# Head of a fused attention and gMLP kernel: block 0 on two queues, K's weights ahead of the first DMA transposes, row sums from a scalar operation

## The chip, the cores and the metric

The kernel runs on one core of a Trainium2 chip. The metric is the device time of one execution in microseconds (us). Lower is better. In this text PE is the matrix engine, DVE the vector engine, ACT the scalar engine, POOL the GpSimd engine and SP the sync engine, which here does nothing but issue DMAs.

## The reference

The input x has 2048 rows of 512 values in bf16. It is normalised row by row, and two branches that read the normalised rows are added to it:

```python
def _A_ref(x, wqkv, wo):                      # H = 32 heads of 16, W = 8 taps, dilation 2
    qkv = (x @ wqkv).reshape(B, S, 3, H, Dh)  # -> q, k, v per head
    idx = pos[:, None] - off[None, :]         # off = 0, 2, ..., 14
    logits = einsum('bhsd,bhswd->bhsw', q, k[idx]) * Dh ** -0.5   # masked where idx < 0
    o = einsum('bhsw,bhswd->bhsd', softmax(logits), v[idx])
    return o @ wo

def _B_ref(x, w_in, w_sp, b_sp, w_out):       # F = 1792, Fh = 896
    z = gelu(x @ w_in)
    z1, z2 = z[..., :Fh], layernorm(z[..., Fh:])
    g = einsum('ts,bsf->btf', w_sp, z2) + b_sp[None, :, None]
    return (z1 * g) @ w_out

xn = layernorm(x)
return x + _A_ref(xn, wqkv, wo) + _B_ref(xn, w_in, w_sp, b_sp, w_out)
```

## The kernel before

The rows are cut into 16 blocks of 128, numbered 0 to 15, and into 4 groups of 512. Every step of the work is a task with an engine, a function that issues its instructions, an assumed duration `est` and the keys that it reads and writes. A planner in the kernel (`Plan.schedule`) walks through the tasks with a model of the engines and gives each engine one fixed order. It uses the `est` values, a model of DMA (`dma_bw`, `dma_lat`), assumed landing times for the first loads (`land`), a tolerance `tol` within which a task of better priority may go first, and `overlap`, the time by which a DVE instruction may start before its predecessor's end. `emit` then writes each engine's instructions in that order with semaphore waits. The order of the first tasks is written out by hand, as lists of names before the call of `plan.schedule` (L1006 to L1015): each name in a list follows the one before it.

The stages, by their lines and task names:

- **Loads.** `ldx0` to `ldx15` bring the blocks of x (L541, L514), `ldwv0` and `ldwv1` the two halves of V's weights (L518), `ldwin2a0`, `ldwin2a1` (L524) and `ldwin2b` (L530) the columns of w_in that make z2, `ldq` and `ldk` the weights of Q and K (L536). A queue issues its DMAs in order. Block 0, block 1 and `ldwin2a0` are issued by ACT, the rest by SP.
- **Warm-up.** `NWARM` matmuls of ones (L561) keep PE busy until the first data are there. Eight have 512 columns, the rest 128.
- **Blocks 0 and 1.** They are not normalised before their first use. DVE sums each row (`sum0`, `sum1`, L592) and subtracts the mean (`cen0`, `cen1`, L594), PE transposes the result (`xTc0_0` to `xTc1_1`, L578), ACT copies it to SBUF (L599), and V and z2 of these blocks are scaled by 1/std as they leave PSUM.
- **Layernorm of every block.** `bnst` (L603), `bnag` (L605) and `vpe` (L609) on DVE, `rstd` on POOL (L621), `norm` on DVE (L637).
- **Transposes of the normalised rows.** Blocks 2 and 3 go through PE (`xTr2`, `xTr3`, L578) and an ACT copy (L627). Blocks 0, 1 and 4 to 15 go by DMA transposes issued on SP (`xTd`, L631).
- **Projections.** V (`V`, L666; its ACT copy L670 and its store by POOL L673), z2 (`z2_b_0`, `z2_b_1`, L770, with its gelu on ACT L775 and sums of squares L780), Q and K (`Qj_c`, `Kj_c`, L682, with the ACT copy L691), z1 (L813).
- **Attention on DVE.** Products (L703, L708), softmax (L733 to L757), products with V (`pv`, L938, L941, L944) and a DMA transpose of each block's result (`OTd`, L947).
- **Spatial mixing and output.** g on PE (L910), its ACT copy (L918) and two DVE operations (L921, L924), then for each block the two output products on PE (L966, L975), the residual on DVE (L981) and the store (L986). For block 15 the output is cut in two parts.

On SP the hand-written order before is `ldq`, `xTd0`, `xTd1`, `ldk`, `ldx8` to `ldx15`. On DVE it is `sum0`, `cen0`, `sum1`, `cen1`, the statistics of blocks 0, 2 and 1, `norm2`, the statistics of block 3, `norm0`, `norm1`, `norm3`. On PE the first projection of Q, `Q0_0`, follows `z2_3_1`.

Of the kernel before, what the change touches and what calls it, by code (L numbers as in the profile page):

```python
# [10 lines left out]
ALU = mybir.AluOpType  # L11
ACTF = mybir.ActivationFunctionType
AX = mybir.AxisListType
# [325 lines left out]
def build_kernel(nc, A_x, A_wqkv, A_wo, B_x, B_w_in, B_w_sp, B_b_sp, B_w_out, out, report=False, emit=True):  # L339
# [3 lines left out]
    NB = S // 128  # L343
# [5 lines left out]
    NVS = 4  # L349
    NPB = 3  # L350
    NXT = 4
    NWARM = 15
    x2 = A_x[0]
    o2 = out[0]

# [3 lines left out]
    off = {}  # L359
# [34 lines left out]
    plan = Plan()  # L394

    with ExitStack() as es:
        ar = es.enter_context(nc.sbuf_tensor("arena", [128, AR], BF))
# [19 lines left out]
        def P(bk, n, o_=0):  # L417
            return ps[:, bk.col(o_): bk.col(o_) + n]
# [62 lines left out]
        def c_act(n, psum=True, accum=False):  # L481
            return (170.0 if psum else 205.0) + n * 0.833 + (200.0 if accum else 0.0)
# [4 lines left out]
        def c_ts(n):  # L487
            return 265.0 + n * 0.27

        T = plan.add  # L490

        def dma(eng, fn, nbytes, chan, reads=(), writes=(), name="", xbar=False, prio=0.0, after=()):
            return T(eng, fn, reads=reads, writes=writes, name=name, prio=prio, after=after,
                     dma=dict(chan=chan, nbytes=nbytes, xbar=xbar))
# [12 lines left out]
          writes=["ident"], est=300, name="ident1")  # L507
# [4 lines left out]
        def ld_x(b, eng="sp"):  # L512
            sl = b
            return dma(eng, lambda e: e.dma_start(A("xin", 512, 512 * sl), x2[128 * b:128 * b + 128, :]), 128 * 512 * 2,  # L514
                ("xin", sl), writes=[("xin", sl)], name="ldx%d" % b)

        def ld_wv(hf):
            dma("sp", lambda e: e.dma_start(AC(off["wv"] + 1024 * hf, [[512, 2], [1, 512]]),  # L518
                                            A_wqkv[256 * hf:256 * hf + 256, 1024:1536].rearrange("(c p) n -> p c n",
                                                                                               p=128)),  # L520
                256 * 512 * 2, ("wv", hf), writes=[("wv", hf)], name="ldwv%d" % hf)

        def ld_win2a(kh, eng):
            dma(eng, lambda e: e.dma_start(  # L524
                AC(off["w_in2"] + 1792 * kh, [[896, 2], [1, 448]]),
                B_w_in[256 * kh:256 * kh + 256, 896:1344].rearrange("(c p) n -> p c n", p=128)),
                256 * 448 * 2, ("w_in2a", kh), writes=[("w_in2a", kh)], name="ldwin2a%d" % kh)
# [7 lines left out]
        def ld_wqk(which, eng):  # L535
# [2 lines left out]
                A_wqkv[:, 512 * which: 512 * which + 512].rearrange("(c p) n -> p c n", p=128)),  # L538
                512 * 512 * 2, ("wqk", which), writes=[("wqk", which)], name="ld%s" % ("qk"[which]))

        dma("act", lambda e: e.dma_start(A("xin", 512), x2[0:128, :]), 128 * 512 * 2, ("xin", 0),  # L541
            writes=[("xin0", 0), ("xin0", 1)], name="ldx0")
        ld_x(1, "act")
        ld_win2a(0, "act")
        ld_wv(0)
        ld_wv(1)
        ld_win2a(1, "sp")
        ld_x(2, "sp")
        ld_x(3, "sp")
        ld_win2b()  # L550
        ld_x(4, "sp")
# [5 lines left out]

        bw = plan.bank("warm")
        for wi in range(NWARM):
            n_ = 512 if wi < 8 else 128  # L560
            T("pe", (lambda bw, n_: lambda t: t.matmul(P(bw, n_), ones[:, 0:128], ones[:, 0:n_], start=True,  # L561
                                                       stop=True))(bw, n_),
              writes=[bw], est=(427.0 if n_ == 512 else 107.0), name="warm%d" % wi, prio=1000)
# [20 lines left out]
        def ln_block(b):  # L584
            sl = b % 8
            xin = A("xin", 512, 512 * b)
            xn = A("xn", 512, 512 * sl)
            xk = [("xin", b)] if b else [("xin0", 0), ("xin0", 1)]

            if b < 2:  # L590
                xc = A("xc", 512, 512 * b)
                T("dve", lambda v: v.tensor_reduce(Fv("sx", 1, b), xin, AX.X, ALU.add), reads=xk, writes=[("sx", b)],  # L592
                  est=685, name="sum%d" % b, prio=-2)
                T("dve", lambda v: v.tensor_scalar(xc, xin, 512.0, Fv("sx", 1, b), ALU.mult, ALU.subtract),  # L594
                  reads=xk + [("sx", b)], writes=[("xc", b)], est=c_ts(512), name="cen%d" % b, prio=-2)
                for hf in range(2):
                    bc = plan.bank("xTc%d_%d" % (b, hf))
                    pe_tr(xc, [("xc", b)], "xTc%d_%d" % (b, hf), bc, (2 * hf, 2 * hf + 1))
                    T("act", (lambda hf, bc: lambda a: a.activation(A("xcT", 256, 512 * b + 256 * hf),  # L599
                                                                    P(bc, 256, 256 * hf), ACTF.Copy,  # L600
                                                                    scale=1.0 / 512))(hf, bc),
                      reads=[bc], writes=[("xcT", b, hf)], est=c_act(256), name="xcT%d_%d" % (b, hf), prio=-1)
            T("dve", lambda v: v.bn_stats(Fv("st6", 6, 6 * b), xin), reads=xk, writes=[("st6", b)],  # L603
              est=685, name="bnst%d" % b, prio=b * 0.1)
# [225 lines left out]
        for b in range(2, NB):  # L830
# [7 lines left out]
          writes=[("KTpad", c) for c in range(4)], est=170, name="ktpad", prio=2, after=lnr[:8])  # L838
# [5 lines left out]
          prio=2, after=lnr[:8])  # L844
# [160 lines left out]
        byname = {t.name: t for t in plan.tasks}  # L1005
        for names in (["warm%d" % wi for wi in range(NWARM - 3)] + ["xTc0_0", "xTc0_1"] +  # L1006
                      ["warm%d" % wi for wi in range(NWARM - 3, NWARM)] +
                      ["V0_0", "xTc1_0", "xTc1_1", "V0_1", "V1_0", "V1_1", "z2_0_0", "z2_1_0", "z2_0_1", "xTr2",
                       "z2_1_1", "V2_0", "V2_1", "xTr3", "z2_2_0", "z2_2_1", "V3_0", "V3_1", "z2_3_0", "z2_3_1", "Q0_0"],
                      ("rstd2", "rstd1", "rstd3", "rstd4", "Vw0"), ["ldq", "xTd0", "xTd1", "ldk"] + ["ldx%d" % b for b in range(8, NB)],  # L1010
                      ("sum0", "cen0", "sum1", "cen1", "bnst0", "bnag0", "vpe0", "bnst2", "bnag2", "vpe2", "bnst1",
                       "bnag1", "vpe1", "norm2", "bnst3", "bnag3", "vpe3", "norm0", "norm1", "norm3", "bnst4"),
                      ["bnst%d" % b for b in range(4, NB)],
                      ("xcT0_0", "xcT0_1", "xcT1_0", "xcT1_1", "Ve0", "xTe2", "Ve1", "z2g0", "xTe3", "z2g1", "Ve2", "z2g2",
                       "z2s0"), ("V10_1", "Q3_3"), ("z2_3_1", "Q0_1"), ("z2_3_1", "Q0_2"), ("z2_3_1", "Q0_3")):  # L1015
            for n0, n1 in zip(names, names[1:]):
                if byname[n0] not in byname[n1].deps:
                    byname[n1].odeps.add(byname[n0])

        plan.schedule(tol=30.0, dma_bw=270.0, dma_lat=1300.0, overlap=0.0,  # L1020
                      land=dict(ldx0=3580.0, ldx1=4750.0, ldwv0=4100.0, ldwv1=5350.0, ldwin2a0=6550.0, ldwin2a1=6600.0, ldx2=7050.0, ldx3=7400.0,
                                ldwin2b=8650.0, ldx4=9050.0, ldx5=9400.0, ldx6=9750.0, ldx7=10200.0, ldq=11700.0,
                                ldk=15000.0))
        if report:
            print("arena", AR, "fp", FR)
            plan.report()
# [47 lines left out]
```

## Time and profile before

| what | value |
|---|---|
| median of 3 runs | 237.98 us (237.9 to 239.03) |
| the profiled execution | 238.3 us, span 237.1 us |
| PE busy | 231.5 us, 98% of the span |
| DVE busy | 215.8 us, 91% |
| ACT busy | 95.2 us, 40% |
| POOL busy | 32.1 us, 14% |
| DMA moved | 44.12 MB, mean 186 GB/s |

The span runs from the first to the last instruction of the program on the core. The profiled execution's own time is 1.2 us longer. All times in rows of the profile are counted from the span's start. A row of the trace's list in order of time gives the start, the duration, the engine, the line, the operation, its output and input, shapes and count, and in square brackets the idle time before it and what ended it. Instructions of one kind that follow each other are merged into a row. A queue that only issues is written with a q (SPq, ACTq, POOLq). Matmuls are pipelined: of 512 columns each has a duration of about 379 ns, but they start closer together than that.

### The profile page before, as it was taken

The page shows a single profiled execution, that of the slowest core. Times are in us where ns is not written, and L with a number is a line of the kernel's source. Part 1 is how long each engine was busy: PE and PEld are TensorE (multiplying, and loading weights), DVE is VectorE, ACT ScalarE, POOL GpSimd, SP SyncE. Part 2 cuts the span into 40 slices and gives each one's busy share as a digit, 9 for nine tenths or more (in the row PEclk, how much of TensorE's full clock was granted, in tenths as well). Part 3 has the DMA queues.
Part 4 walks back from the last instruction along what each step waited for, and adds up shares of the span by engine and source line. Part 5 has one row for each costly group of instructions (what it writes and reads, how often), then busy time and mean ns, then how long its engine had stood idle before and what let it go on. Part 6 is the DMA issues. An engine that isn't in the chain of part 4 may idle for free.

```text
span 237.1 us, 2958 instructions
## 1 busy us (share of the span) xinstructions
PE 231.5 (98%) x1109; PEld 108.5 (46%) x1130; DVE 215.8 (91%) x269; ACT 95.2 (40%) x141; POOL 32.1 (14%) x56
## 2 busy tenths in 40 slices
PE   8998999999999999999999999999999999999996
PEld 3444455555444444444444444444444444444443
DVE  4787989999997899999999999999989998999982
ACT  3496889988986896601113411111111111000000
POOL 1476381401634000000000000000000000000000
DMA  6979869998147239014299999999899866393443
GB/s 205 304 205 259 205 135 197 142 230 187 66 152 249 60 116 115 0 33 144 66 358 230 225 231 185 296 173 316 274 212 271 293 189 195 76 320 118 145 139 129
DMA packets 83117, 44.12 MB, mean 186 GB/s; under 512 B 55440, under 2 KB 82464, under 8 KB 83104
## 3 DMA queue, kind: packets, MB, share of 16 engines
q1 hardware_dynamic: 81600, 41.30, 70.7%
q0 software_dynamic: 800, 2.11, 2.3%
q10 hardware_dynamic: 704, 0.52, 0.7%
q8 instruction: 9, 0.15, 0.2%
q14 instruction: 4, 0.03, 0.1%
HBM read 26.35 MB, written 4.21 MB: 129 GB/s over the span
## 4 chain that ended last, share of the span: by engine, by line
PE 90%; DMA 4%; DVE 3%; issue 1%; SPq 1%; ACT 0%; POOL 0%; DVEq 0%
PE ps L910 41%; PE ps L682 11%; PE ps L813 10%; PE ps L975 10%; PE ps L770 8%; PE ps L966 6%; PE ps L666 4%; DMA arena<-in_A_x_dram 2%; DMA arena<-in_A_wqkv_dram 2%; DVE fpool L603 1%; ACT arena L775 0%; PE ps L718 0%; SPq L518 0%; DVE arena L981 0%; DVE fpool L605 0%
## 5 line engine op out<-in xcount | busy, mean ns | idle before, releaser
L910 PE MATMUL ps<-arena 128*128 128x512 bf16 x439 | 96.6, 379 | 0.5
L910 PEld LDWEIGHTS ps<-arena 128*128 128x128 bf16 x448 | 43.7, 98 | 53.1 <-issue 0.4
L918 ACT ACTIVATE arena<-ps 128x1024 bf16<-128x1024 f32 (+1 forms) x16 | 14.7, 916 | 75.3 <-PE ps L910 75.3
L703 DVE TENSOR_TENSOR arena<-arena 128x4096 bf16<-128x4096 bf16 x16 | 36.5, 2288 | 0.2
L938 DVE TENSOR_TENSOR arena<-arena 128x4096 bf16<-128x4096 bf16 x16 | 36.5, 2284 | 0.0
L941 DVE TENSOR_TENSOR arena<-arena 128x2048 bf16<-128x2048 bf16 (+1 forms) x32 | 30.6, 958 | 1.0
L682 PE MATMUL ps<-arena 128*128 128x512 bf16 x126 | 28.9, 379 | 1.3 <-DMA arena<-in_A_wqkv_dram 1.2
L708 DVE TENSOR_TENSOR arena<-arena 128x4096 bf16<-128x4096 bf16 x12 | 27.5, 2290 | 0.3
L975 PE MATMUL ps<-arena 128*128 128x512 bf16 (+2 forms) x117 | 26.9, 366 | 0.1
L770 PE MATMUL ps<-arena 128*128 128x448 bf16 x128 | 26.0, 352 | 0.0
L813 PE MATMUL ps<-arena 128*128 128x512 bf16 x110 | 24.4, 379 | 0.1
L682 PEld LDWEIGHTS ps<-arena 128*128 128x128 bf16 x128 | 14.3, 113 | 14.7 <-DMA arena<-in_A_wqkv_dram 1.7
L691 ACT ACTIVATE arena<-ps 128x1024 bf16<-128x1024 f32 x16 | 16.3, 1021 | 5.3 <-PE ps L682 5.0
L770 PEld LDWEIGHTS ps<-arena 128*128 128x128 bf16 x128 | 12.4, 98 | 11.7 <-DMA arena<-in_B_w_in_dram 0.2
L975 PEld LDWEIGHTS ps<-arena 128*128 128x128 bf16 x119 | 11.4, 98 | 12.8
L813 PEld LDWEIGHTS ps<-arena 128*128 128x128 bf16 x112 | 10.9, 98 | 13.3 <-ACT arena L819 0.3
L966 PE MATMUL ps<-arena 128*128 128x512 bf16 (+2 forms) x66 | 16.5, 366 | 0.1
L819 ACT ACTIVATE arena<-ps 128x1024 bf16<-128x1024 f32 (+1 forms) x16 | 13.9, 922 | 4.9 <-PE ps L813 4.9
L666 PE MATMUL ps<-arena 128*128 128x512 bf16 x60 | 15.2, 379 | 0.7 <-ACT arena L599 0.3
L780 ACT ACTIVATE arena<-arena 128x896 bf16<-128x896 bf16 x16 | 15.1, 946 | 0.1
L775 ACT ACTIVATE arena<-ps 128x896 bf16<-128x896 f32 x14 | 12.8, 915 | 3.3 <-PE ps L770 3.3
L981 DVE TENSOR_TENSOR arena<-ps,arena 128x512 bf16<-128x512 f32 (+2 forms) x17 | 10.4, 653 | 3.3 <-PE ps L975 2.8
(61 smaller groups left out, 168.8 us busy)
## 6 DMA issues: line engine op xcount, KB each, us to landing
arena<-vscr SPq DMA_DIRECT2D x16, 1024.0 KB, 6.0
arena<-in_A_x_dram SPq DMA_DIRECT2D x30, 128.0 KB, 4.1
vscr<-arena POOLq DMA_DIRECT2D x16, 128.0 KB, 2.3
out_dram<-arena SPq DMA_DIRECT2D x15, 128.0 KB, 2.0
arena<-in_A_wqkv_dram SPq DMA_DIRECT2D x2, 512.0 KB, 5.1
arena<-in_B_w_in_dram SPq DMA_DIRECT2D x1, 896.0 KB, 5.4
arena<-in_B_w_out_dram SPq DMA_DIRECT2D x1, 896.0 KB, 5.0
arena<-arena SPq DMA_TRANSPOSE x34, 2.9
```

The costliest lines, as they stand in the source:

```text
L666: last = t.matmul(P(bk, 512), xTv(b, dc), A("wv", 512, 512 * dc), start=(dc == 0), stop=(dc == 3))
L682: last = t.matmul(P(bk, 512, 512 * which), AC(off["wqk"] + 2048 * which + 512 * dc + c, [[4, 128]]), AC(off["xnT"] + dc * S + 512 * j, [[1 ...
L691: T("act", lambda a: a.activation(AC(qo, [[ko - qo, 2], [1, 512]]), P(bk, 1024).rearrange("p (t n) -> p t n", t=2), ACTF.Copy, scale=0.5), ...
L703: T("dve", (lambda pbv, qb, kb: lambda v: v.tensor_tensor(pbv, qb, kb, ALU.mult))(pbv, qb, kb), reads=rd, writes=[("pb", s_)], est=c_tt(40 ...
L708: T("dve", (lambda av, bv: lambda v: v.tensor_tensor(av, av, bv, ALU.add))(av, bv), reads=[("pb", 1)], writes=[("pb", acc)], est=c_tt(4096 ...
L770: last = t.matmul(P(bk, 448, 512 * hf), xTv(b, dc), AC(off["w_in2"] + 896 * dc + 448 * hf, [[1, 448]]), start=(dc == 0), stop=(dc == 3))
L813: last = t.matmul(P(bk, 512, 512 * i), AC(off["w_in1"] + 896 * dc + 128 * fc, [[1, 128]]), AC(off["xnT"] + dc * S + 512 * j, [[1, 512]]), ...
L910: last = t.matmul(P(bk, 512, 512 * i), AC(off["z2"] + FH * sh + 128 * fc, [[1, 128]]), AC(off["wT%d" % r_] + sh * 512, [[1, 512]]), start= ...
L938: T("dve", lambda v: v.tensor_tensor(tv, tv, av, ALU.mult), reads=[("attn", b)], writes=[("Vs", sv)], est=c_tt(4096), name="pv%d" % b, pri ...
L941: T("dve", (lambda n: lambda v: v.tensor_tensor(A("Vs", n, 4096 * sv), A("Vs", n, 4096 * sv), A("Vs", n, 4096 * sv + n), ALU.add))(n), wri ...
L966: last = t.matmul(P(bk, cn), AC(off["OT"] + 512 * tb + 128 * cc, [[1, 128]]), AC(off["wo"] + 512 * cc + c0, [[1, cn]]), start=(cc == 0), s ...
L975: last = t.matmul(P(bk, cn), AC(off["z1T"] + fc * S + 128 * tb, [[1, 128]]), AC(off["w_out"] + 512 * fc + c0, [[1, cn]]), start=False, sto ...
```

## The change

- Block 0's load is cut in two halves of 64 rows. `ldx0_0` is issued by ACT, `ldx0_1` by SP ahead of V's weights.
- `ldx2` is issued ahead of `ldwin2a1`.
- `sum0` and `sum1` are no longer a reduction. They are a multiply by one and an add of zero over the row, with the row's sum as second output. The first output goes to the tile that `cen0` and `cen1` then overwrite.
- `ldk` is issued right behind `ldq`, ahead of `xTd0` and `xTd1`.
- `norm0` moves up on DVE, from behind the statistics of block 3 to ahead of those of block 1. `rstd0` is named first in POOL's order.
- Two warm-up matmuls fewer: one of 512 columns and one of 128.
- The planner's numbers are new: `tol`, `dma_bw`, `dma_lat`, `overlap` and the assumed landing times.

```diff
-    NWARM = 15
+    NWARM = 13
...
-        dma("act", lambda e: e.dma_start(A("xin", 512), x2[0:128, :]), 128 * 512 * 2, ("xin", 0),
-            writes=[("xin0", 0), ("xin0", 1)], name="ldx0")
+        for hf, eng in ((0, "act"), (1, "sp")):
+            dma(eng, (lambda hf: lambda e: e.dma_start(ar[64 * hf:64 * hf + 64, off["xin"]: off["xin"] + 512],
+                                                       x2[64 * hf:64 * hf + 64, :]))(hf),
+                64 * 512 * 2, ("xin0", hf), writes=[("xin0", hf)], name="ldx0_%d" % hf)
         ld_x(1, "act")
         ld_win2a(0, "act")
         ld_wv(0)
         ld_wv(1)
+        ld_x(2, "sp")
         ld_win2a(1, "sp")
-        ld_x(2, "sp")
...
-            n_ = 512 if wi < 8 else 128
+            n_ = 512 if wi < 7 else 128
...
-                T("dve", lambda v: v.tensor_reduce(Fv("sx", 1, b), xin, AX.X, ALU.add), reads=xk, writes=[("sx", b)],
-                  est=685, name="sum%d" % b, prio=-2)
+                T("dve", lambda v: v.tensor_scalar(xc, xin, 1.0, 0.0, ALU.mult, ALU.add, accum_out=Fv("sx", 1, b)), reads=xk, writes=[("sx", b), ("xc", b)],
+                  est=410, name="sum%d" % b, prio=-2)
...
-                      ("rstd2", "rstd1", "rstd3", "rstd4", "Vw0"), ["ldq", "xTd0", "xTd1", "ldk"] + ["ldx%d" % b for b in range(8, NB)],
-                      ("sum0", "cen0", "sum1", "cen1", "bnst0", "bnag0", "vpe0", "bnst2", "bnag2", "vpe2", "bnst1",
-                       "bnag1", "vpe1", "norm2", "bnst3", "bnag3", "vpe3", "norm0", "norm1", "norm3", "bnst4"),
+                      ("rstd0", "rstd2", "rstd1", "rstd3", "rstd4", "Vw0"),
+                      ["ldq", "ldk", "xTd0", "xTd1"] + ["ldx%d" % b for b in range(8, NB)],
+                      ("sum0", "cen0", "sum1", "cen1", "bnst0", "bnag0", "vpe0", "bnst2", "bnag2", "vpe2", "norm0",
+                       "bnst1", "bnag1", "vpe1", "norm2", "bnst3", "bnag3", "vpe3", "norm1", "norm3", "bnst4"),
...
-        plan.schedule(tol=30.0, dma_bw=270.0, dma_lat=1300.0, overlap=0.0,
-                      land=dict(ldx0=3580.0, ldx1=4750.0, ldwv0=4100.0, ldwv1=5350.0, ldwin2a0=6550.0, ldwin2a1=6600.0, ldx2=7050.0, ldx3=7400.0,
-                                ldwin2b=8650.0, ldx4=9050.0, ldx5=9400.0, ldx6=9750.0, ldx7=10200.0, ldq=11700.0,
-                                ldk=15000.0))
+        plan.schedule(tol=5.0, dma_bw=250.0, dma_lat=1600.0, overlap=30.0,
+                      land=dict(ldx0_0=2700.0, ldx0_1=3050.0, ldx1=3650.0, ldwv0=4350.0, ldwv1=5250.0, ldwin2a0=6300.0,
+                                ldwin2a1=6850.0, ldx2=5800.0, ldx3=7250.0, ldwin2b=8400.0, ldx4=8750.0, ldx5=9100.0,
+                                ldx6=9450.0, ldx7=9800.0, ldq=11300.0, ldk=12800.0))
```

More of the change, by code (lines that the diff above doesn't have):

```diff
@@ L1009, in build_kernel @@
                        "z2_1_1", "V2_0", "V2_1", "xTr3", "z2_2_0", "z2_2_1", "V3_0", "V3_1", "z2_3_0", "z2_3_1", "Q0_0"],
-                      ("rstd2", "rstd1", "rstd3", "rstd4", "Vw0"), ["ldq", "xTd0", "xTd1", "ldk"] + ["ldx%d" % b for b in range(8, NB)],
-                      ("sum0", "cen0", "sum1", "cen1", "bnst0", "bnag0", "vpe0", "bnst2", "bnag2", "vpe2", "bnst1",
-                       "bnag1", "vpe1", "norm2", "bnst3", "bnag3", "vpe3", "norm0", "norm1", "norm3", "bnst4"),
+                      ("rstd0", "rstd2", "rstd1", "rstd3", "rstd4", "Vw0"),
+                      ["ldq", "ldk", "xTd0", "xTd1"] + ["ldx%d" % b for b in range(8, NB)],
+                      ("sum0", "cen0", "sum1", "cen1", "bnst0", "bnag0", "vpe0", "bnst2", "bnag2", "vpe2", "norm0",
+                       "bnst1", "bnag1", "vpe1", "norm2", "bnst3", "bnag3", "vpe3", "norm1", "norm3", "bnst4"),
                       ["bnst%d" % b for b in range(4, NB)],
-                      ("xcT0_0", "xcT0_1", "xcT1_0", "xcT1_1", "Ve0", "xTe2", "Ve1", "z2g0", "xTe3", "z2g1", "Ve2", "z2g2",
-                       "z2s0"), ("V10_1", "Q3_3"), ("z2_3_1", "Q0_1"), ("z2_3_1", "Q0_2"), ("z2_3_1", "Q0_3")):
+                      ("xcT0_0", "xcT0_1", "xcT1_0", "xcT1_1", "Ve0", "xTe2", "Ve1", "z2g0", "xTe3",
+                       "z2g1", "Ve2", "z2g2", "z2s0"), ("V10_1", "Q3_3"), ("z2_3_1", "Q0_1"), ("z2_3_1", "Q0_2"),
+                      ("z2_3_1", "Q0_3")):
             for n0, n1 in zip(names, names[1:]):
```

## The prediction

> **What bounds the kernel now.** I read the page first, then PE's waits, then the list in order of time around each wait.
>
> ```profile
> PE 231.5 (98%) x1109; PEld 108.5 (46%) x1130; DVE 215.8 (91%) x269; ACT 95.2 (40%) x141; POOL 32.1 (14%) x56
> ```
> ```profile
> PE ps L682 <- DMA arena<-in_A_wqkv_dram: 1.2, 1, 1.2
> PE ps L561 <- PEq L1059: 0.8, 1, 0.8
> PE ps L666 <- ACT arena L599: 0.3, 1, 0.3
> PE ps L666 <- issue: 0.2, 1, 0.2
> PE ps L666 <- ACT arena L775: 0.2, 1, 0.2
> ```
>
> PE bounds the whole span, and its work is fixed, so the time is that work plus PE's idle time. A row here gives total, count and longest. Of 2.7 us of waits, 1.2 are one wait of K's projection for K's weights. Apart from the last of them, all lie in the first 19 us, where this change works:
>
> ```profile
> 0.84 3.93 PE L561 MATMUL ps<-const-bfloat16-1.0 128*128 128x512 bf16 x12 [0.84 <-PEq L1059]
> ...
> 3.50 0.69 DVE L592 TENSOR_REDUCE fpool<-arena 128x1 f32<-128x512 bf16 x1 [2.31 <-DMA arena<-in_A_x_dram]
> ...
> 4.22 0.35 DVE L594 TENSOR_SCALAR arena<-arena,fpool 128x512 bf16<-128x512 bf16 x1
> ...
> 4.72 0.38 PE L578 MATMUL ps<-arena 128*128 128x128 bf16 x4
> ...
> 7.46 0.69 DVE L603 BATCH_NORM_STATS2 fpool<-arena 128x6 f32<-128x512 bf16 x1 [0.89 <-DMA arena<-in_A_x_dram]
> 7.62 2.43 PE L770 MATMUL ps<-arena 128*128 128x448 bf16 x12
> ...
> 9.03 0.58 PEld L770 LDWEIGHTS ps<-arena 128*128 128x128 bf16 x4 [0.18 <-DMA arena<-in_B_w_in_dram]
> ...
> 9.48 0.40 DVE L637 TENSOR_SCALAR arena<-arena,fpool 128x512 bf16<-128x512 bf16 x1
> ...
> 11.24 2.59 SPq L631 DMA_TRANSPOSE arena<-arena  x2
> 11.26 0.81 PE L666 MATMUL ps<-arena 128*128 128x512 bf16 x3 [0.16 <-issue]
> ...
> 12.12 0.23 PEld L578 LDWEIGHTS ps<-arena 128*128 128x128 bf16 x4 [0.55 <-DVE arena L637]
> ...
> 13.88 0.58 SPq L536 DMA_DIRECT2D arena<-in_A_wqkv_dram  x1
> ...
> 14.50 4.02 SPq L514 DMA_DIRECT2D arena<-in_A_x_dram  x8
> ...
> 16.25 1.03 PE L682 MATMUL ps<-arena 128*128 128x512 bf16 x4
> ...
> 18.45 3.86 PE L682 MATMUL ps<-arena 128*128 128x512 bf16 x17 [1.18 <-DMA arena<-in_A_wqkv_dram]
> ...
> 18.74 0.69 DVE L603 BATCH_NORM_STATS2 fpool<-arena 128x6 f32<-128x512 bf16 x1 [1.53 <-DMA arena<-in_A_x_dram]
> ```
>
> SP issues `ldk` only at 13.88, behind two transposes that wait for the late `norm0` and `norm1`; PE does `Q0_0` at 16.25 and then stands until 18.45.
>
> **The wait for K's weights.** How much PE loses there, and when `ldk` can land, come from these rows (PE's pace in a full stretch; DMA in four stretches):
>
> ```profile
> 26.22 7.07 PE L682 MATMUL ps<-arena 128*128 128x512 bf16 x32
> 33.13 6.22 PE L770 MATMUL ps<-arena 128*128 128x448 bf16 x32
> ```
> ```profile
> 2.00:2.75 0.75, 0.75 (x3) 0.30 (x2) 0.00 (x0) 0.52 (x1) 0.00 (x0) 1.00 0.67 205
> 2.75:5.50 2.75, 2.53 (x15) 1.23 (x13) 1.93 (x5) 1.44 (x4) 0.00 (x0) 1.00 0.98 326
> 5.50:11.00 5.50, 5.44 (x32) 2.56 (x32) 4.33 (x15) 2.16 (x6) 1.81 (x4) 1.00 1.06 349
> 11.00:12.40 1.40, 1.18 (x9) 0.59 (x10) 1.28 (x4) 1.40 (x3) 1.16 (x2) 1.00 0.07 23
> ```
>
> From 26.22 to 33.13 there are 32 matmuls, 0.216 us each. `Q0_0` is four, 0.86 us. From 16.25 to 18.45 are 2.20 us, so 1.34 us are lost. The last two numbers of each window are DMA's busy share and GB/s: saturated up to 11, almost idle (0.07) from 11.0 to 12.4. After the change `ldk` is issued right behind `ldq`, before that hole. Its 512 KB (0.524 MB) at 349 GB/s take 1.50 us; even started at the hole's end, 12.4, they land by about 13.9 where `K0_0` needs them at about 17.1 (16.25 + 0.86). The cover is 3 us, so the whole 1.34 us goes. SP issues one DMA more ahead (half of block 0, about 0.5 us by the x8 row, 4.02 / 8); DMA's saturation from 2.75 on hides that.
>
> What moves with it: `xTd0` and `xTd1` now queue behind 512 KB more, and `Q0_0` needs both. `norm0` now comes ahead of the row of 9.48, but `norm1` stays behind block 3's statistics, so `xTd1` is still issued near 11.2. Bounds for its landing: the 2.4 to 2.9 us of before and the up to 5.1 us that transposes took behind loads:
>
> ```profile
> DMA to landing us min/median/max: 2.4/2.6/2.9
> ```
> ```profile
> DMA to landing us min/median/max: 3.4/4.3/5.1
> ```
>
> The first row is the two at 11.24, the second three issued behind the eight loads of 14.50. That gives 13.6 to 16.3. I take 14.3, since only `ldk` is ahead, landed by 13.9. `Q0_0` will want to start at about 16.1, so it is covered; at the far end 0.2 us would be lost. The eight x loads follow at about 12.5 instead of 14.50; DVE's wait of 1.53 us at 18.74 goes too, which keeps DVE ahead of an earlier PE.
>
> **The start of block 0.** The split can only bring the landing forward from 3.50. The sum of a row as second output isn't in the trace. From below it is the plain scalar operation (L594), 0.35 us; from above the reduction (L592), 0.69, plus a read of the accumulator as ACT has it behind its own sums:
>
> ```profile
> 12.33 0.21 ACT L775 ACTIVATION_READ_ACCUMULATOR arena<-ps,fpool 128x1 f32 x1
> ```
>
> that is 0.35 to 0.90. I take 0.69: like the reduction it must add 512 values of a row. Anywhere in that range the step is worth little, because of what is late next. The Trainium skill's page "SBUF — State Buffer", section "Who interferes with whom", says that the form of this operation that also writes out its accumulator cannot enter the fast two-port modes; by that this step saves nothing, and no run here shows it. PE's start hangs on the chain load, sum, centre, transpose, V, and the two early ends of it can move by up to some 0.5 us together. But `z2_0_0` at 7.62 needs `ldwin2a1`, now behind `ldx2`, and `z2_0_1` needs `ldwin2b`:
>
> ```profile
> 1.82 0.46 SPq L524 DMA_DIRECT2D arena<-in_B_w_in_dram  x1
> ...
> 3.31 0.43 SPq L530 DMA_DIRECT2D arena<-in_B_w_in_dram  x1
> ```
> ```profile
> DMA to landing us min/median/max: 5.3/5.3/5.4
> ```
> ```profile
> DMA to landing us min/median/max: 5.7/5.7/5.7
> ```
>
> The landing rows are of these two issues. The first is `ldwin2a1`: 1.82 + 5.4 = 7.2. It changes places with block 2, which lands just before 7.46; so it will land there, 0.15 us before PE wants it now. The second is `ldwin2b`: 3.31 + 5.7 = 9.0. The weight load of 9.03 already waited for it by 0.18 us. The same bytes stand ahead of it after the change, so PE's head start is used up at 9.03. It survives only if all DMA runs earlier: from 2.00 to 2.75 the share is 0.67, so a fuller start gives at most 0.33 x 0.75 = 0.25 us. I take zero, range 0 to 0.25. With nothing of it gained and the sum at 0.90, the chain is 0.2 us late, which is what the waits of 11.26 and 12.12 absorb. The two warm-up matmuls left out only make room.
>
> **Block 2 ahead of `ldwin2a1`, `norm0` moved up.** The load for block 3's transpose stood idle 0.55 us at 12.12 behind DVE. On PE itself: three matmuls from 11.26 at 0.216 end at 11.91, and the next weights are loaded at 12.12, so 0.2 us is lost. DVE's chain to there begins with block 2 at 7.46 and is gapless. `ldx2` gains at most 224 KB at 349 GB/s, 0.66 us, at least about 0.1 (loads of both queues interleave); I take 0.55. `norm0` now lies in that chain, 0.40 us (the row of 9.48). `norm2` and all behind it: 0.15 us earlier, range -0.3 to 0.26. In the order of DVE `bnst1`, `bnag1`, `vpe1`, `norm2` wait behind `norm0`, and `norm0` for `rstd0`, which POOL has long done. Gain on PE: 0.15 us.
>
> **Sum.** 1.34 + 0 + 0.15 = 1.5 us (1.49). From the profiled 238.3 that gives 236.8; the median of 237.98 is 0.3 lower than the profiled time, so I predict 236.5. Own range of this case 236.0 (all of the 0.25, and 0.2 of the small waits) to 236.9 (block 2's chain 0.3 later). A change under 0.5%, 1.19 us, I call none, about what a measurement of this kernel can tell: the limits are 236.79 and 239.17.
>
> **Rivals.**
>
> *The head gives nothing.* Block 0 lands at 3.50 as before, because its halves share DMA engines that other loads fill, and `norm0` eats block 2's lead. For it: DMA is saturated from 2.75. Against it: it is not before that. Only K's 1.34 is left: 236.6. 10%. The Trainium skill's page "DMA: Bandwidth & Descriptors", section "Rules for kernel authors", has a rule for this: of two transfers to disjoint halves of the partitions it says "Don't bother", since both use the same engines. By it block 0 gains nothing.
>
> *Late transposes.* `Q0_0` takes over part of K's wait, for `xTd1`. For it: the 5.1 us row; if SP is held up by half a microsecond more behind its fuller queue, it lands at 16.9, 0.8 late: 237.3. Against it: `ldk` has landed well before. 10%.
>
> *A cold clock.* The first twelve warm-ups, eight of 512 columns and four of 128, took 3.93 us, 0.44 for each 512 columns, where later matmuls take 0.216: PE runs at half pace until about 4.7. If the earlier and thinner start puts that off by as long again, the 2.2 us of work from 4.72 to 7.62 (eight transposes of 128 columns at 0.054, eight V matmuls at 0.216) takes 2.2 us more, less 0.4 of waits there: 1.8 lost, about 238.3. 6%.
>
> *Slower: DVE's new order holds the last block.* PE's last product waits for the last DMA transpose of the attention result:
>
> ```profile
> 197.81 0.42 DVE L921 TENSOR_TENSOR arena<-arena 128x512 bf16<-128x512 bf16 x1 [0.50 <-ACT arena L918]
> ...
> 198.61 2.28 DVE L938 TENSOR_TENSOR arena<-arena 128x4096 bf16<-128x4096 bf16 x1
> ...
> 203.26 1.88 DVE L981 TENSOR_TENSOR arena<-ps,arena 128x512 bf16<-128x512 f32 x3
> ```
> ```profile
> 228.75 1.19 SPq L947 DMA_TRANSPOSE arena<-arena  x1
> ...
> 232.59 0.81 PE L966 MATMUL ps<-arena 128*128 128x384 bf16 x4
> ```
>
> It is issued at 228.75. With the 2.4 to 2.9 us of the transposes at 11.24 it lands at about 231.3; PE wants it at 232.59, a cover of 1.3 us. The planner's new `tol` and `overlap` order all later work anew, and 30 ns on each of 269 DVE instructions shift its model by up to 8 us. If one more product with V (198.61 to 203.26, 4.65 us) comes to lie behind 197.81, the transpose is 4.65 later, 3.3 beyond the cover: 236.5 + 3.3 = 239.8. It ends slower than before once more than 2.8 us (1.3 + 1.49) are moved there. Against it: DVE's idle times of 0.50 at 197.81 and 1.53 at 18.74 leave room, and DVE's later waits are for PE and ACT, which come earlier too. 14%.
>
> **How the numbers follow.** Forecast 60%, head nothing 10%, late transposes 10%, cold clock 6%, slower 14%. Faster by over 0.5%: 0.56 of the forecast's 0.60 and 0.06 of the 0.10 that lies at the limit, 0.62. Within: the 0.04 and 0.04 left, 0.10 and most of the clock's 0.06, 0.22. Slower: 0.14 and what is left of the clock, 0.16. The range from 235.8 (0.2 under the own range, for a run on the quick side) to 238.9 holds all cases but most of the slower one.
>
> **What would show it.** Right: `Q0_0` and `K0_0` without a gap; `ldk` landed before 14.5; the first z2 at 7.4 to 7.6 however early the first transposes are; the list of PE's waits after 20 us as short as now; the last OT transpose landed ahead of PE. Wrong: a wait of L682 for a transpose or L966 for a DMA; the second output under 0.5 or over 0.9 us makes its step wrong, not the sum; `z2_0_1` well before 9.0 makes the head's zero wrong.

## The result, and the profile after

The changed kernel takes 237.26 us (median of 22 runs, 236.94 to 239.26), the kernel before beside it 238.06 us. The ratio is 0.9969 [0.996, 0.9978]: shorter by 0.31%, about 0.75 us. The interval lies below 1, but the gain is under the 0.5% from which the prediction speaks of a change. The forecast was 0.63%, 1.49 us, so half of the gain is missing. The profiled execution takes 237.5 us with a span of 235.9; before it was 238.3 with 237.1. The span lost 1.2 us, the whole time only 0.8.

The page's row of engines after, and the list of PE's waits (us in total, times, longest):

```profile
PE 232.1 (98%) x1128; PEld 108.4 (46%) x1128; DVE 207.9 (88%) x271; ACT 94.8 (40%) x141; POOL 32.8 (14%) x56
```
```profile
PE ps L580 <- DVE arena L596: 0.9, 2, 0.4
PE ps L563 <- PEq L1063: 0.8, 1, 0.8
PE ps L668 <- ACT arena L601: 0.2, 1, 0.2
```

K's wait of 1.2 us is gone, and what the list of before had later in the span too. New are two waits of the transposes at the start (L580) for DVE's centred blocks. Lines behind L541 stand two higher than before. The list in order of time shows the start:

```profile
0.80 0.59 SPq L542 DMA_DIRECT2D arena<-in_A_x_dram  x1
...
0.81 0.57 ACTq L542 DMA_DIRECT2D arena<-in_A_x_dram  x1
...
1.43 0.84 ACTq L514 DMA_DIRECT2D arena<-in_A_x_dram  x1
1.44 1.08 SPq L518 DMA_DIRECT2D arena<-in_A_wqkv_dram  x2
...
3.52 0.69 DVE L594 TENSOR_SCALAR_CACHE_REDUCE arena<-arena 128x512 bf16<-128x512 bf16 x1 [2.32 <-DMA arena<-in_A_x_dram]
...
4.06 0.44 SPq L530 DMA_DIRECT2D arena<-in_B_w_in_dram  x1
...
4.13 0.08 DVE L594 DVE_READ_ACCUMULATOR arena<-arena 128x1 f32 x1
4.25 0.35 DVE L596 TENSOR_SCALAR arena<-arena,fpool 128x512 bf16<-128x512 bf16 x1
...
5.38 0.69 DVE L594 TENSOR_SCALAR_CACHE_REDUCE arena<-arena 128x512 bf16<-128x512 bf16 x1 [0.78 <-DMA arena<-in_A_x_dram]
...
6.52 0.40 PE L580 MATMUL ps<-arena 128*128 128x128 bf16 x4 [0.42 <-DVE arena L596]
...
8.22 1.25 PEld L772 LDWEIGHTS ps<-arena 128*128 128x128 bf16 x8 [0.40 <-DMA arena<-in_B_w_in_dram]
8.23 2.51 PE L772 MATMUL ps<-arena 128*128 128x448 bf16 x12
...
9.80 0.49 PEld L772 LDWEIGHTS ps<-arena 128*128 128x128 bf16 x4 [0.33 <-DMA arena<-in_B_w_in_dram]
...
16.63 7.07 PE L684 MATMUL ps<-arena 128*128 128x512 bf16 x32
...
233.44 0.55 PE L977 MATMUL ps<-arena 128*128 128x128 bf16 x7
```

Block 0 is there no earlier than before: DVE starts on it at 3.52 (before 3.50). Both halves took 0.57 to 0.59 us to issue, block 1's load behind them 0.84, and everything further back in both queues goes out later: `ldwin2b` (L530) at 4.06 instead of 3.31. Block 1's sum starts at 5.38 after a wait for its load (before at 4.49 without a wait), the first z2 at 8.23 (before 7.62), and `Q0_0` at 16.63, 0.38 us later than before. From there all 32 matmuls of Q and K are one row of 7.07 us: no gap. The rows of before for block 1's load and its sum:

```profile
1.26 0.46 ACTq L514 DMA_DIRECT2D arena<-in_A_x_dram  x1
...
4.49 0.68 DVE L592 TENSOR_REDUCE fpool<-arena 128x1 f32<-128x512 bf16 x1
```

The stretches of DMA (us, busy share and GB/s are the last two numbers) show a hole after, between 3.0 and 3.5, that before does not have; after comes first:

```profile
3.00:3.50 0.50, 0.50 (x3) 0.23 (x2) 0.00 (x0) 0.50 (x1) 0.00 (x0) 1.00 0.59 111
```
```profile
3.00:3.50 0.50, 0.50 (x3) 0.22 (x2) 0.00 (x0) 0.50 (x1) 0.00 (x0) 1.00 1.06 367
```

The account goes by three marks: `Q0_0`'s start, the last product's row on PE, and the time around the span (a run's time less its span). The row of before:

```profile
234.60 0.55 PE L975 MATMUL ps<-arena 128*128 128x128 bf16 x7
```

- Up to `Q0_0`: 16.25 to 16.63, 0.38 us lost. The first z2 is 0.61 late; from it to `Q0_0` it is 8.40 us instead of 8.63, so 0.23 come back.
- From there to the last row: 218.35 (234.60 - 16.25) to 216.81 (233.44 - 16.63), 1.54 gained: 1.34 of K's wait and 0.20 of small waits, such as that for L775.
- Around the span: median of the 22 runs 1.57 us, beside 1.2 before; 0.3 to 0.4 lost.

Together 0.8, the difference of the two profiled executions.

### The profile page after: what moved, and what is told of

It reads as the page before. It is cut to its first block, busy times and chain, and to the rows that moved or that the text cites. A ratio compares the mean times of both kernels' runs of the same rounds, so it can differ in the third digit from the quotient of the medians.

```text
span 235.9 us, 2986 instructions
## 1 busy us (share of the span) xinstructions
PE 232.1 (98%) x1128; PEld 108.4 (46%) x1128; DVE 207.9 (88%) x271; ACT 94.8 (40%) x141; POOL 32.8 (14%) x56
## 4 chain that ended last, share of the span: by engine, by line
PE 96%; DMA 2%; DVE 1%; ACTq 0%; issue 0%; DVEq 0%
PE ps L912 41%; PE ps L684 12%; PE ps L772 10%; PE ps L815 10%; PE ps L977 10%; PE ps L668 6%; PE ps L968 6%; DMA arena<-in_A_x_dram 2%; PE ps L720 1%; DVE arena L983 0%; PE ps L580 0%; DVE arena L594 0%; ACTq L542 0%; DVE arena L596 0%; DVEq L319 0%
## 5 line engine op out<-in xcount | busy, mean ns | idle before, releaser
L684 PEld LDWEIGHTS ps<-arena 128*128 128x128 bf16 x128 | 14.5, 113 | 13.0
L983 DVE TENSOR_TENSOR arena<-ps,arena 128x512 bf16<-128x512 f32 (+2 forms) x17 | 11.1, 657 | 10.0 <-PE ps L977 10.0
L693 ACT ACTIVATE arena<-ps 128x1024 bf16<-128x1024 f32 x16 | 16.3, 1021 | 5.9 <-PE ps L684 5.7
L923 DVE TENSOR_TENSOR arena<-arena 128x1024 bf16<-128x1024 bf16 (+1 forms) x16 | 10.0, 624 | 7.7 <-ACT arena L920 7.7
L668 PE MATMUL ps<-arena 128*128 128x512 bf16 x64 | 16.1, 380 | 0.2 <-ACT arena L601 0.2
L821 ACT ACTIVATE arena<-ps 128x1024 bf16<-128x1024 f32 (+1 forms) x16 | 13.9, 919 | 4.9 <-PE ps L815 4.7
```

The source lines that it names most:

```text
L668: last = t.matmul(P(bk, 512), xTv(b, dc), A("wv", 512, 512 * dc), start=(dc == 0), stop=(dc == 3))
L684: last = t.matmul(P(bk, 512, 512 * which), AC(off["wqk"] + 2048 * which + 512 * dc + c, [[4, 128]]), AC(off["xnT"] + dc * S + 512 * j, [[1 ...
L693: T("act", lambda a: a.activation(AC(qo, [[ko - qo, 2], [1, 512]]), P(bk, 1024).rearrange("p (t n) -> p t n", t=2), ACTF.Copy, scale=0.5), ...
```

## The experiments

Where a ratio is given it is to the kernel before, run beside it on the same chip.

**K's order alone**, on the kernel before (`k_order`):

```diff
-["ldq", "xTd0", "xTd1", "ldk"]
+["ldq", "ldk", "xTd0", "xTd1"]
-ldk=15000.0
+ldk=13400.0
```

> The kernel before, with K's weights issued ahead of the first two DMA transposes and nothing else changed (PE's and DVE's orders stay as they were). Theory A (K's wait is the whole gain of the change and the start gives some of it back): PE's gap before the first K matmuls goes from 1.34 us to under 0.1, Q0_0 still starts at about 16.25, the span falls by 1.2 to 1.4 us, the time to about 236.7. Rival B (the gain cannot be had by itself, since the transposes behind K's weights make Q0_0 late): Q0_0 starts later than 16.7 and the time falls by under 0.8 us.

Measured 237.67 us, 0.9973 [0.9961, 0.9985]. The median span falls by 0.8 us, where theory A had 1.2 to 1.4; the late `Q0_0` of the rival does not come either. `Q0_0` and `K0_0` run without a gap, from 16.30, but a new wait comes up:

```profile
16.30 7.07 PE L682 MATMUL ps<-arena 128*128 128x512 bf16 x31
23.20 1.68 PE L770 MATMUL ps<-arena 128*128 128x448 bf16 x8
25.35 0.81 PE L682 MATMUL ps<-arena 128*128 128x512 bf16 x3 [0.47 <-DMA arena<-arena]
...
233.74 0.56 PE L975 MATMUL ps<-arena 128*128 128x128 bf16 x7
```

The old plan puts only eight z2 matmuls ahead of the next group of Q; PE arrives there earlier by all of K's wait and stands for DMA transposes. From `Q0_0` to the last row it is 217.44, 0.91 less than before and 0.63 more than after. So the order alone brings 0.91 of the 1.54; the new plan, with twelve z2 matmuls at that place, brings the rest.

**Block 0 whole again** (`nosplit`) and **the reduction again** (`reduce`), each on the kernel after, with all orders as there:

```diff
-        for hf, eng in ((0, "act"), (1, "sp")):
-            dma(eng, ... 64 * 512 * 2, ... name="ldx0_%d" % hf)
+        dma("act", lambda e: e.dma_start(A("xin", 512), x2[0:128, :]), ... name="ldx0")
```
```diff
-T("dve", lambda v: v.tensor_scalar(xc, xin, 1.0, 0.0, ALU.mult, ALU.add, accum_out=Fv("sx", 1, b)), ...
+T("dve", lambda v: v.tensor_reduce(Fv("sx", 1, b), xin, AX.X, ALU.add), ...
```

> The changed kernel with block 0 loaded whole by ACT again; the planner's orders of PE, DVE and POOL stay those of the changed kernel. Theory A (the DMA added at the head of both queues holds back the whole stream of loads): SP's first issue falls from 0.59 to about 0.45 us, block 1 lands at about 4.4 in place of 5.4, w_in's columns for z2 land 0.6 to 0.8 us earlier, the first z2 starts at about 7.6 in place of 8.23, Q0_0 at about 16.0, and the time falls by 0.5 to 0.7 us to about 236.6. Rival B (the second output of the sum, or w_in behind block 2, holds the head back): the first z2 stays later than 8.0 and the time stays within 0.2 us of the changed kernel's 237.26.

> The changed kernel with the row sums of blocks 0 and 1 as a reduction again (all orders stay). Theory A: the second output costs 0.69 + 0.08 us against 0.69 for the reduction, and DVE waits for block 1 anyway, so the time stays within 0.15 us of the changed kernel's 237.26. Rival B (the sum's form is what delays PE's start): the first transposes come over 0.2 us earlier and the time falls by over 0.3 us.

`nosplit`: 236.80 us, 0.9933 [0.9919, 0.9946], clearly under the kernel after; its median span is 235.3 us, that of after 235.7. The time is near theory A's, but the marks in the profiled execution are not: block 1's sum starts at 5.16, the first z2 at 7.94 and `Q0_0` at 16.28, where about 4.4, 7.6 and 16.0 were expected. `reduce`: 237.15 us, 0.9958 [0.9936, 0.9981], which overlaps it. With the reduction the span is no shorter (median 235.9, after 235.7), but the time around it is back from 1.57 to 1.27. The groups of DVE by line (count | busy us, mean ns | idle before) say why the sum itself brings nothing, after and before:

```profile
L594 DVE TENSOR_SCALAR_CACHE_REDUCE arena<-arena 128x512 bf16<-128x512 bf16 x2 | 1.4, 686 | 3.1 <-DMA arena<-in_A_x_dram 3.1
L594 DVE DVE_READ_ACCUMULATOR arena<-arena 128x1 f32 x2 | 0.2, 82 | 0.0
```
```profile
L592 DVE TENSOR_REDUCE fpool<-arena 128x1 f32<-128x512 bf16 x2 | 1.4, 683 | 2.3 <-DMA arena<-in_A_x_dram 2.3
```

**The row halves alone**, on the kernel before (`split_only`; the reverse of the first diff above):

> The kernel before with block 0's load split over ACT and SP and nothing else changed (PE's and DVE's orders stay). Theory A (the split costs): block 0 lands less than 0.2 us earlier, block 1 about 0.9 us later, the first z2 starts 0.4 to 0.6 us later than 7.62. K's weights are issued behind the transposes as before, so the wait for K takes part of the delay: the time rises by 0.2 to 0.6 us. Rival B (the split alone is harmless and something else delays the loads): the first z2 stays within 0.15 us of 7.62 and the time within 0.15 us of the kernel before. The time around the span is to be read too: 1.2 us in the kernel before, 1.6 in the changed one.

238.48 us, 1.0006 [0.9997, 1.0014]: the rise of 0.2 to 0.6 us does not come, and the median span is no longer than that of before (237.05 and 237.2). In the profiled execution the first z2 starts 0.57 us later (8.19) and `Q0_0` 0.28 us later (16.53), but K's first matmul, which still waits for K's weights, only 0.16 us later than before:

```profile
16.53 1.03 PE L682 MATMUL ps<-arena 128*128 128x512 bf16 x4
18.61 1.70 PE L682 MATMUL ps<-arena 128*128 128x512 bf16 x7 [1.05 <-DMA arena<-in_A_wqkv_dram]
```

So a delay at the start is mostly hidden while K's wait stands. How much of this delay is the halves' cannot be read from this execution, in which PE also ran longer at half pace (last section): in `split_pool` below, which has the same halves, `Q0_0` starts at 16.27 and K's wait ends at 18.45, as before. The time around the span rose here too, to 1.44, with no second output in the kernel.

**Neither of the two** (`neither`: `nosplit` and `reduce` together), and from it **block 2 behind `ldwin2a1` again** (`w_first`):

```diff
-        ld_x(2, "sp")
         ld_win2a(1, "sp")
+        ld_x(2, "sp")
```

> The changed kernel with block 0 loaded whole by ACT and with the row sums as reductions; left of the change are K's weights ahead of the transposes, block 2 ahead of w_in, the moved norm0, two warm-ups fewer and the planner's new numbers. Theory A (the split holds back the loads, and the time around the span is larger only in the kernels with the second output): the span stays at the 235.3 us of the kernel without the split, the time around it falls from 1.5 to 1.25 us, so the time is about 236.5, 0.8% under the kernel before. Rival B (the time around the span does not go with the second output): the time stays at 236.8 or above.

> As the kernel with neither split nor second output, and with w_in's second quarter ahead of block 2 again as in the kernel before. Theory A (block 2's place is worth little, since the next z2 waits for w_in): the time is within 0.2 us of that kernel. Rival B (block 2 early is what lets PE's order run through): the time rises by over 0.3 us, with a wait of PE for DVE's norm of block 2 or 3.

`neither`: 236.68 us, 0.9928 [0.9916, 0.994]. Without the halves and the second output the change brings more than twice what it did. Its list in order of time:

```profile
0.80 0.97 SPq L518 DMA_DIRECT2D arena<-in_A_wqkv_dram  x2
0.80 0.42 ACTq L541 DMA_DIRECT2D arena<-in_A_x_dram  x1
1.26 0.45 ACTq L514 DMA_DIRECT2D arena<-in_A_x_dram  x1
...
7.51 2.43 PE L772 MATMUL ps<-arena 128*128 128x448 bf16 x12
...
15.84 1.89 PE L684 MATMUL ps<-arena 128*128 128x512 bf16 x8
...
232.64 0.55 PE L977 MATMUL ps<-arena 128*128 128x128 bf16 x7
```

`Q0_0` starts at 15.84, and from there to the last row are 216.80 us, as after (all kernels with the new plan have 216.80 or 216.81 here, `tiny` 216.97): all that differs lies ahead of `Q0_0` and around the span. `w_first`: 236.94 us, 0.9946 [0.9931, 0.996]; its median span is 0.25 us longer, which is block 2's worth here, though the intervals overlap. This lies between what the theory and the rival had. As the rival said, weight loads of PE wait for DVE's norms, 0.29 and 0.55 us.

**What of the halves costs: an issue more, or their form.** One kernel puts a 4 KB load of 16 rows, which nothing reads, first on SP (`tiny`); one cuts block 0 by columns (`colsplit`, with the second output; `col_reduce`, with the reduction); one puts an unused load of 64 whole rows first on SP, block 0 whole on ACT (`head64`).

```diff
+dma("sp", lambda e: e.dma_start(ar[0:16, off["tiny"]: off["tiny"] + 128], x2[0:16, 0:128]), ...    # tiny
+dma("sp", lambda e: e.dma_start(ar[0:64, off["tiny"]: off["tiny"] + 512], x2[1984:2048, :]), ...   # head64
-e.dma_start(ar[64 * hf:64 * hf + 64, ...], x2[64 * hf:64 * hf + 64, :])
+e.dma_start(A("xin", 256, 256 * hf), x2[0:128, 256 * hf:256 * hf + 256])                           # colsplit, col_reduce
```

> As the kernel with neither split nor second output, with one more DMA of 4 KB at the head of SP's queue (its data are not used). Theory A (what the split costs is SP's issue time at the head, not bytes): V's weights are issued 0.4 to 0.5 us later, w_in's columns land 0.3 to 0.5 us later, the first z2 starts 0.2 to 0.5 us later and the time rises by 0.2 to 0.5 us. Rival B (the stream of loads is held back by the form of the split loads or by the bytes, not by an issue): the landings of w_in and the time stay within 0.15 us.

> The changed kernel with block 0 in two halves of 256 columns over all 128 rows, in place of two halves of 64 rows; the two queues stay. Theory A (a DMA at the head of SP's queue costs its issue time whatever its form, and loads of 64 rows take longer to issue, 0.58 in place of 0.45 us): the issues fall to about 0.45 us, the third issue on SP comes at about 1.85 in place of 2.08, and the time falls by 0.1 to 0.3 us from the changed kernel. Rival B (the two queues stand in each other's way whatever the form): issues stay at 0.57 us or more, the time within 0.15 us of the changed kernel.

> As the kernel with neither split nor second output, with one more DMA of 64 rows by 512 columns (64 KB, not used) at the head of SP's queue, in place of the 4 KB of the run before; block 0 stays whole on ACT. Theory A (a load of 64 rows of 1 KB is slow to issue and holds back what is issued behind it): SP's first issue takes 0.55 us or more, w_in's columns land 0.3 to 0.7 us later than with the 4 KB, and the time is 0.3 to 0.6 us above its 236.54. Rival B (it is slow only when ACT issues such a load at the same time): issue at 0.40 to 0.46 us, and only the bytes count, 64 KB at 349 GB/s, 0.19 us: the time within 0.25 us of 236.54.

> The changed kernel with block 0 in two halves of 256 columns on the two queues and with the row sums as reductions. Theory A: the span stays at the 235.4 us of the halves by columns with the second output, the time around it falls from 1.6 to about 1.25 us (309 DVE instructions), the time is about 236.65, 0.6 us under the changed kernel and within 0.15 us of the best so far (236.54). Rival B (the second output's first instruction gives DVE something that the reduction doesn't): the span rises by over 0.2 us.

`tiny`: 236.54 us, 0.9923 [0.991, 0.9936]; the theory that one more issue at the head of SP costs time falls. `colsplit`: 236.99, 0.9945 [0.9931, 0.9959]. `col_reduce`: 236.54, 0.9922 [0.9906, 0.9937]. `head64`: 237.25, 0.9952 [0.9934, 0.9971], 0.7 us more than `tiny`, though nothing waits for its load; its 64 KB at 349 GB/s would be 0.19. Its interval just touches those of `tiny` and `col_reduce`, but ten of its twelve runs are longer than the longest of either. The issues, in `head64` and then in `col_reduce`:

```profile
0.80 0.58 SPq L543 DMA_DIRECT2D arena<-in_A_x_dram  x1
...
1.21 0.45 ACTq L514 DMA_DIRECT2D arena<-in_A_x_dram  x1
1.43 1.08 SPq L518 DMA_DIRECT2D arena<-in_A_wqkv_dram  x2
```
```profile
0.80 0.40 SPq L542 DMA_DIRECT2D arena<-in_A_x_dram  x1
0.81 0.40 ACTq L542 DMA_DIRECT2D arena<-in_A_x_dram  x1
1.24 0.45 ACTq L514 DMA_DIRECT2D arena<-in_A_x_dram  x1
1.25 0.93 SPq L518 DMA_DIRECT2D arena<-in_A_wqkv_dram  x2
...
3.01 0.69 DVE L594 TENSOR_REDUCE fpool<-arena 128x1 f32<-128x512 bf16 x1 [1.82 <-DMA arena<-in_A_x_dram]
```

It is the load of 64 rows that issues slowly, 0.58 us by itself against 0.40, and V's two weight loads behind it on its queue take 1.08 instead of 0.93. Whether the loss comes from the slow issue or from how the data then flow is not separated: `ldwin2b` goes out 0.43 us later in `tiny` than in `neither` (3.73, 3.30) at no cost, and only 0.33 later still in `head64` (4.06). The profiled execution of `head64` is the longest of its twelve, 239.34 us, and not typical. Block 1 came early in it, but V's weights late, and PE fell back to half pace: six V matmuls in 2.76 us, in the kernel after in 1.56.

```profile
6.88 0.64 PE L668 MATMUL ps<-arena 128*128 128x512 bf16 x2 [2.29 <-DMA arena<-in_A_wqkv_dram]
...
7.75 2.76 PE L668 MATMUL ps<-arena 128*128 128x512 bf16 x6
```

The column halves issue in 0.40, and DVE starts on block 0 at 3.01, in kernels that cut it by rows at 3.45 to 3.55. That is not the columns' doing, for `tiny` has a whole block 0 as early:

```profile
3.06 0.69 DVE L594 TENSOR_REDUCE fpool<-arena 128x1 f32<-128x512 bf16 x1 [1.86 <-DMA arena<-in_A_x_dram]
```

What the two have in common is that V's weights go out behind another load on SP. The earlier block 0 is worth little, as forecast: `neither`, where DVE starts on it at 3.47, takes 236.68 us against their 236.54, with intervals that overlap.

**Where the loss arises.** In these profiled executions DVE waits for block 1's load before block 1's sum (times in us):

| kernel | block 0 | block 1's sum | first z2, after that sum | `Q0_0`, after that z2 |
|---|---|---|---|---|
| after | rows | 5.38 | 2.85 | 8.40 |
| reduce | rows | 5.71 | 2.77 | 8.39 |
| split_pool | rows | 5.11 | 2.77 | 8.39 |
| colsplit | columns | 4.76 | 2.78 | 8.34 |
| col_reduce | columns | 4.88 | 2.77 | 8.33 |
| nosplit | whole | 5.16 | 2.78 | 8.34 |
| tiny | whole | 4.62 | 2.77 | 8.33 |

So once block 1 is late, PE's start follows its sum at a fixed distance, and w_in's late loads add at most 0.15 us (0.08 and 0.07, after). With rows block 1's sum starts at 5.11 to 5.71, with columns or a whole block at 4.62 to 5.16; this is one execution each, and they overlap. That the row halves cost time rests on the median spans, 0.40 us from `nosplit` to after and 0.45 from `neither` to `reduce`.

**The time around the span.** It had risen in four kernels (after, `nosplit`, `split_only`, `colsplit`). They had in common more instructions on DVE: the trace lists 309 there before (the page's 269 and those that only wait or signal) and 308 in the new plan without halves and second output (`neither`). The halves, which need a second wait, add one; the second output adds its two reads. Two kernels test that count alone: `neither` with three memsets of one column more (`dve_plus3`), and `split_only` with DVE's one memset of zeros on POOL (`split_pool`).

```diff
+[T("dve", ... v.memset(Fv("dum", 1, i), 0.0) ...) for i in range(3)]      # dve_plus3
-T("dve", lambda v: v.memset(zeros, 0.0), ...)                             # split_pool
+T("pool", lambda v: v.memset(zeros, 0.0), ...)
```

> As the kernel with neither split nor second output, with three more DVE instructions (one-column memsets that nobody reads, in DVE's idle time before block 0). So far the time around the span was 1.20 to 1.27 us in the kernels with 308 or 309 DVE instructions in their trace, 1.44 to 1.5 with 310, 1.57 to 1.6 with 311. Theory A (that time goes with the number of DVE instructions): the span stays within 0.1 us of 235.45, the time around it rises from 1.23 to about 1.6, the time to about 237.0. Rival B (it goes with the second output itself or with the split): it stays at 1.20 to 1.27, the time at 236.7.

> The kernel before with block 0 split by rows, as run above, and the first memset of zeros moved from DVE to POOL, which leaves 309 DVE instructions in place of 310. Theory A (number of DVE instructions): the time around the span falls from 1.44 to about 1.25 us and the time by 0.2 us, to about 238.3. Rival B (the split itself): it stays at 1.44.

| kernel | DVE instructions | around the span, median us |
|---|---|---|
| neither, tiny, w_first, head64 | 308 | 1.23, 1.24, 1.26, 1.26 |
| before, k_order, reduce, col_reduce, split_pool | 309 | 1.25, 1.24, 1.27, 1.28, 1.23 |
| split_only, nosplit | 310 | 1.44, 1.51 |
| after, colsplit, dve_plus3 | 311 | 1.57, 1.60, 1.60 |

(Before stood between 1.21 and 1.25 in the runs beside.) `dve_plus3` takes 237.10 us, 0.9947 [0.9929, 0.9965]: with the span of `neither` (235.5 and 235.45) it is 0.4 us slower, all of it around the span. `split_pool` takes 238.15, 0.9991 [0.9981, 1.0001], 0.2 around the span less than `split_only`, with the same work, one instruction of it on another engine. So the time around the span goes with the number of DVE instructions in this program, in a step between 309 and 311. What the chip does in that time isn't in the trace, which begins after it or ends before it; this stays open.

`tiny` and `col_reduce` are the fastest kernels run, 0.7 us under the kernel after by the medians and 1.1 us by the ratios; `neither`, simpler, is within their intervals.

## Why the prediction was half right

**K's wait: right in size and cause.** All 1.34 us went. But with the old plan the order alone brings only 0.91 of the 1.54 us behind `Q0_0` (`k_order`), since a wait for transposes comes up; that the rest needs the new plan I had not seen. The lines of the times from issue to landing after, first for `ldq` and `ldk` (L536), then for the two transposes (L633), give the landings:

```profile
DMA to landing us min/median/max: 6.4/6.8/7.3
```
```profile
DMA to landing us min/median/max: 3.9/5.0/6.1
```

`ldk`, issued at 7.2, landed at 14.5, not by 13.9; the transposes at 14.9 and 15.4, not 14.3, still within the forecast's 13.6 to 16.3 and ahead of `Q0_0`. In `neither`, without the late start, `ldk` landed at about 13.

**The head's term: this step failed.** The sum had 0 for the start, with a range of 0 to 0.25, because "the split can only bring the landing forward", and half a microsecond of SP's issue that "DMA's saturation from 2.75 on hides". The first is true of block 0 alone, and brought nothing (3.52). The second priced the added issue by a load of 128 rows and looked only at SP's queue. What I left out is block 1's load, behind the other half on ACT's queue: it went out 0.17 us later, took 0.84 us to issue instead of 0.46, and landed 3.9 us after its issue began instead of 3.1 (the two lines below, after first). So block 1's sum started 0.89 us later than before and the first z2 0.61 us later, where the sum had nothing. I had seen PE's limit in w_in's loads. They were late too (`ldwin2b` landed at 9.8, 4.06 + 5.7, not 9.0), but added 0.15 us at most. DMA, which I had taken to be full from 2.75, fell to a share of 0.59 between 3.0 and 3.5; this alone is not the loss, for `col_reduce` has 0.66 there. `Q0_0` came 0.38 late where I had it 0.15 early: 0.53 us of the missing gain. `tiny` shows that a plain issue more is hidden, as I said; the row halves are not. Part of block 1's delay is this one execution: the landing took 3.5 to 4.3 us with row halves and 2.8 to 3.6 without, but 3.9 in `nosplit` too. By the median spans the halves cost 0.40 us. Why their data are late was not found.

```profile
DMA to landing us min/median/max: 3.9/3.9/3.9
```
```profile
DMA to landing us min/median/max: 3.1/3.1/3.1
```

With the halves undone the head comes out as forecast. Since all from `Q0_0` on takes the same time, the median spans of `nosplit` (235.3, profiled 235.5 with `Q0_0` at 16.28) and `neither` (235.45, profiled 235.2 with 15.84) put their `Q0_0` at about 16.1 by my estimate, which is what I had. The first z2 of single executions scatters, without any load of 64 rows, from 7.39 (`tiny`) to 7.96 (`k_order`), so 7.51 in `neither` within my 7.4 to 7.6 is partly luck.

**The time around the span: left out.** I took the profiled time less the span, 1.2 us, to be a constant. It rose by 0.3 to 0.4, the second piece of the missing gain. The two pieces, 0.53 and 0.32 (1.57 - 1.25), less the 0.20 of small waits that I had only as range, are 0.65 of the 0.7 that is missing. By the medians the halves' 0.40 and the 0.32 make 0.72.

**The second output: right, and worth nothing.** I took 0.69 from between 0.35 and 0.90; it is 0.69 and a read of 0.08, of which the chain sees 0.73 from start to the centring, against 0.72 before. What I cited of the Trainium skill, page "SBUF — State Buffer", section "Who interferes with whom", that this form gets no fast mode, agrees with the 686 ns beside the reduction's 683 and the 0.35 us of the plain scalar operation.

**Block 2 first and `norm0`: right in sign.** I had 0.15, range -0.3 to 0.26. From the first z2 to `Q0_0` it is 8.63 us before, 8.40 after, 8.33 in `neither` and 8.59 in `w_first`: with the new orders block 2's place is worth 0.26, as by the spans. In the kernel after the term cannot be told apart, for `k_order` and `split_only`, with the old orders, take 8.34 too when their first z2 is as late as 7.96 and 8.19.

**The rivals.** "The head gives nothing" came nearest, but did not go far enough: the head cost time. Of the Trainium skill's "Don't bother" for two partition halves (page "DMA: Bandwidth & Descriptors", section "Rules for kernel authors") I had made a gain of nothing; the runs show a loss, 0.40 and 0.45 us in the median spans of after and `reduce` against `nosplit` and `neither`, while halves by columns (`col_reduce`) neither gain nor lose. Late transposes did not stop `Q0_0`, but in `k_order` they stop the next group: the mechanism was there, one group later than I looked, and the new plan covers it. The clock did not turn colder in the profiled execution: PE's transposes ran at full pace from 4.74. The slower rival, DVE's new order at the end, did not come: no wait of PE after 20 us is left in the list.

## What to carry to other kernels

Before splitting a load to have it sooner, look at what is issued behind it on the same queues, and at which load PE waits for next: here that was block 1, not block 0, and with the row halves it came later (5.38 instead of 4.49, in one execution each). An added issue may be hidden by what flows already, as in `tiny`; price it by a load of its own form, and not, as I did, by one of another. And compare whole times as well as spans: a shorter span can be paid for outside it.

## What was not expected of the hardware

- A load of 64 rows of 1 KB took 0.57 to 0.59 us to issue, one of 128 rows of 1 KB, also first on its queue, 0.37 to 0.43, 128 rows of 512 B 0.39 to 0.41, 16 rows of 256 B 0.40. Behind the first, block 1's load took 0.84 or 0.85 instead of 0.45. Why 64 rows are slow was not found.
- The time around the span rose from 1.25 to 1.45 to 1.6 us with 309, 310 and 311 instructions on DVE.
- PE's half pace at the start had ended by 4.7 us in the profiles of before and after (four transposes in 0.38 us), but in that of `split_only` only between 6.4 and 6.8 (four transposes at 6.43 in 0.54, the six V matmuls at 6.80 in 1.56), without a change to the warm-ups between before and `split_only`. One profile's start is therefore good to some tenths of a microsecond only; the verdicts above rest on the medians and ratios.
